# Sinkhorn attention and a residual MLP on one core: q of two batches turned by DMA transposes, v and k mixing moved to other slots, and the last output tile split by columns

## The chip, the core and the metric

The kernel runs on one core of one Trainium2 chip. A core has TensorE (PE, the matmuls; PEld is its weight load), VectorE (DVE), ScalarE (ACT), GpSimd (POOL) and SyncE (SP), which here only issues DMAs. Each works through its own instructions in order and waits on semaphores for the others. The DMAs that SyncE, ScalarE and GpSimd issue are carried out by the core's 16 DMA engines. The metric is the time of one execution on the device in microseconds. Eight runs of the kernel before have a median of 276.93 us (276.42 to 279.34).

## What is computed

Four batches of 768 positions go through an attention with 8 heads of 64, whose blocks of keys and values are first mixed by an 8x8 matrix per head (five Sinkhorn rounds of a softmax over rows and columns), and then through a token mixing layer and a channel MLP, both with residuals:

```python
    P = sort_net
    for _ in range(5):
        P = np.exp(P - np.max(P, axis=-1, keepdims=True))
        P = P / (np.sum(P, axis=-1, keepdims=True) + 1e-09)
        P = P / (np.sum(P, axis=-2, keepdims=True) + 1e-09)
    k_sorted = np.einsum('bhij,bhjcd->bhicd', P, k_b)      # 8 blocks of 96 positions
    v_sorted = np.einsum('bhij,bhjcd->bhicd', P, v_b)
    # within each block i of 96 queries, keys and values:
    attn = softmax(scale * q_b @ k_sorted^T)
    x = attn @ v_sorted                                    # (4, 768, 512) over all heads
    a1 = alpha1 * x + beta1
    u = x + lam * einsum('ts,bsd->btd', w_tok, a1)         # token layer
    a2 = alpha2 * u + beta2
    out = u + lam * (np.maximum(a2 @ w_ch1, 0.0) @ w_ch2)  # channel layer, 512 -> 2048 -> 512
```

(The first lines are put together from the reference's steps; the arithmetic is the reference's.) Inputs and output are float32. The kernel works in 16-bit formats with float32 sums.

## The kernel before

**The order is written out by hand.** Every engine object is wrapped so that its instructions keep the order in which the program issues them (class `Engine`, L55 to L71); SyncE's DMAs alone are issued without the wrapper. The backbone is the loop at L859: for each batch b and each half hf of its 768 positions there is an *h phase* and then a *c phase*. I write h(b,hf) and c(b,hf). An h phase has 16 units (`h_unit`, L692): four matmuls give a 128x384 tile of the hidden layer, and ACT applies Relu and writes it to `hTa` or `hTb`. A c phase has three output tiles kk of 128 positions, each in four quarters of four matmuls (`ch_unit`, L695); after the last quarter DVE multiplies by `lamB`, GpSimd (for the last half of batch 3, DVE) adds `u`, and SyncE writes the tile to `out` in two DMAs, of 96 and of 32 rows. The tile goes through `ost`, which has two buffers, shared over the whole kernel.

**All other work hangs on this backbone.** `put(b, hf, kind, n, ...)` (L791) notes a piece of work for after unit n of a phase (n runs to 15 in an h phase and to 11 in a c phase), and `run` issues it there, in the order in which it was noted. While batch p = b-1 passes through the channel layer, batch b's attention and token layer are made:

- `load_kv(b)` and `load_q(b)` on GpSimd's queue: four DMAs of v and k (6 KB pieces into `raw`, two buffers) and six of q (`qn`, one buffer), all with a change of type.
- `mix_matrix(b)`: one small matmul (`repv_ps`) and six DVE operations give the mixing matrices.
- `mix_v(b, n)`, three times: two matmuls each into `mix_ps`, and a copy of 128x1024 into `mixed`. `bounce_v(b)` writes `mixed` to DRAM in two DMAs, and `back_v(b)` reads it back into `Vs` with positions on partitions, in pieces of 128 bytes.
- `mix_k(b, n)`, three times: eight matmuls into `kmix_ps`, and four casts into `kT`, on ACT or DVE.
- `q_turn_late(b, g)`, four times: six PE transposes of `qn` into `qt_ps` and a copy into `qT`.
- `score(b, g, hf)`, eight times: eight matmuls into `sc_ps`, and an exp on ACT into `et`. `pv(b, g, hf)`, eight times: eight matmuls into `x_ps`, a reciprocal and a multiplication on DVE into `x`; the first affine step of the token layer (`a1 = alpha1*x + beta1`, two DVE operations) is kept back in the list `late` and issued by `flush`.
- `tails(b)`: six small DVE copies that move the last quarter of the positions onto partitions 96 to 127. `moe_tok(b, kt)`, six times: six matmuls and three elementwise operations (`toktmp`, `u16`, and `u` in float32 on GpSimd). `moe_cross(b, hf)`: three DMA transposes of `u16` into `uT` on SyncE's queue. `moe_affine(b, hf)`: four DVE operations that give `a2T`, what the next h phase multiplies.

PSUM is held by two pools: `psA` (two buffers of two banks: scores, pv, mixing of v and k, `repv_ps`) and `psB` (four buffers of one bank: h, ch, tok and qt tiles). A tile takes the buffer that was freed first in program order, so a matmul can wait for the last reader of an earlier tile of any kind in that pool.

In the kernel before, batch b's v is mixed in h(b-1,0), k is mixed and q turned in c(b-1,0), the scores of batches 2 and 3 run from quarter 8 of c(b-1,0) into h(b-1,1), one to three pieces at a slot, and the first three token tiles stand together in c(b-1,1).

Of the kernel before, what the change touches and what calls it, by code (L numbers as in the profile page):

```python
# [7 lines left out]
FT = mybir.dt.float32  # L8
F16 = mybir.dt.float16
# [7 lines left out]
def kernel(  # L17
# [56 lines left out]
    dve = Engine(nc.vector)  # L74
    act = Engine(nc.scalar)
    pool = Engine(nc.gpsimd)

    dram = ctx.enter_context(tc.tile_pool(name="dram", bufs=1, space=bass.MemoryType.DRAM))
    wts = ctx.enter_context(tc.tile_pool(name="wts", bufs=1))
# [9 lines left out]
    def psb(shape, dtype, name):  # L89
        return pools["psB"].tile(shape, dtype, name=name, tag="psB")  # L90
# [263 lines left out]
    def mix_matrix(b):  # L354
        mix_values(b, psa)
        big = att.tile([128, 2, H * NB], F16, name="bigM", tag="bigM", bufs=3)
        dve.tensor_tensor(
            big[:], bigV[b][:].rearrange("p h i -> p (h i)").unsqueeze(1).to_broadcast([128, 2, H * NB]),
            mth[:].unsqueeze(2).to_broadcast([128, 2, H * NB]), ALU.mult,
        )  # L360
        bigM[b] = big
        bgp = att.tile([128, 2, 2, H4, NB], F16, name="bigP", tag="bigP", bufs=3)
        for th in range(2):
            dve.tensor_tensor(
                bgp[:, :, th, :, :], bigV[b][:].rearrange("p (g a) i -> p a g i", a=2),
                mth[:, th:th + 1].unsqueeze(2).unsqueeze(3).to_broadcast([128, 2, H4, NB]), ALU.mult,
            )
        bigP[b] = bgp
# [91 lines left out]
    def pv(b, g, hf):  # L460
        if g == 0 and hf == 0:
            x_of[b] = moep.tile([128, 8, C], F16, name="x128", tag="x128", bufs=2)
            a1_of[b] = moep.tile([128, 8, C], F16, name="a1", tag="a1", bufs=1)
        ps = psa([128, 2, 512], FT, "x_ps")[:].rearrange("p a (k d) -> p a k d", d=128)
        et = ets[(b, g, hf)][:].rearrange("p a i t -> p (a i t)")
        for ii in range(4):
            for h2 in range(2):
                lo = (4 * h2 + ii) * BLK
                w = min(128, 8 * BLK - lo)
                pe.matmul(  # L470
                    ps[0:w, h2, ii, 0:D + 1], et[0:BLK, lo:lo + w],
                    Vs[b % 2][0:BLK, (2 * g + h2) * NB + 4 * hf + ii, 0:D + 1], start=True, stop=True,
                )
        rc = att.tile([128, 2, 4], FT, name="rcb", tag="rc", bufs=3)
        dve.reciprocal(rc[0:BLK], ps[0:BLK, :, :, D])
        dve.tensor_tensor(
            x_of[b][0:BLK, 4 * hf:4 * hf + 4, g * 128:(g + 1) * 128].rearrange("p k (a d) -> p k a d", a=2),
            ps[0:BLK, :, :, 0:D].rearrange("p a k d -> p k a d"),
            rc[0:BLK].rearrange("p a k -> p k a").unsqueeze(3).to_broadcast([BLK, 4, 2, D]), ALU.mult,
        )  # L480
        flush()
        late.append(lambda: first_affine(b, slice(0, BLK), slice(4 * hf, 4 * hf + 4), slice(g * 128, (g + 1) * 128)))

    late = []

    def flush():
        while late:
            late.pop()()

    def tails(x, lo, hi, eng):  # L490
        flush()
        for a in range(3):
            eng(x[96:128, a:a + 4:3, lo:hi], x[32 * a:32 * a + 32, 6:8, lo:hi])

    def q_turn_late(b, g, eng):
        if g == 0:
# [45 lines left out]

    def bounce_v(b):
        for th in range(2):
            nc.sync.dma_start(
                vscr[b, :, th * HB:(th + 1) * HB, :], mixed[b][th * 64:(th + 1) * 64, :, :],
            )

    def back_v(b):
        nc.sync.dma_start(Vs[b % 2][0:BLK, :, 0:D], vscr[b].rearrange("x t d -> t x d"))  # L550

    w_tokT = const([128, NT, S], F16, "w_tokT")
    wp_of = {}
# [106 lines left out]
    def moe_cross(b, hf):  # L660
        uT = uT_of[(b, hf)] = att.tile([128, CT, 384], F16, name="uT", tag="uT", bufs=2)
        for m in range(3):
            nc.sync.dma_start_transpose(
                uT[:, :, m * 128:(m + 1) * 128], u16_of[b][:, 3 * hf + m, :],
            )

    def moe_affine(b, hf):
        for ci in range(CT):
            affine(b, hf, ci, uT_of[(b, hf)][:, ci, :], dve)
# [22 lines left out]
    def h_unit(b, hf, m):  # L692
        h_part(b, hf, m, range(CT))

    def ch_unit(b, hf, kk, part=(0, HT)):  # L695
        hT = hT_of[(b, hf)]
        kt = 3 * hf + kk
        if part[0] == 0:
            ch_of[0] = psb([128, C], FT, "ch_ps")
        cps = ch_of[0]  # L700
        for m in range(*part):
            pe.matmul(
                cps[:], hT[m][:, kk * 128:(kk + 1) * 128], W2p[:, m, :],
                start=(m == 0), stop=(m == HT - 1),
            )
        if part[1] < HT:
            return
        ost = att.tile([128, C], FT, name="ost", tag="ost", bufs=2)
        dve.tensor_tensor(ost[:], cps[:], lamB[:], ALU.mult)
        (dve if b == B - 1 and hf == 1 else pool).tensor_tensor(ost[:], ost[:], u_of[b][kt], ALU.add)  # L710
        act_out(out[b, kt * 96:(kt + 1) * 96, :], ost[0:96, :])
        act_out(out[b, TAIL + kt * 32:TAIL + (kt + 1) * 32, :], ost[96:128, :])

    ch_of = {}
    act_out = nc.sync.dma_start

    copy = dve.tensor_copy

# [72 lines left out]
    def put(b, hf, kind, n, *todo):  # L791
        at.setdefault((b, hf, kind, n), []).extend(todo)
# [6 lines left out]
        put(0, 0, "h", 4 + kt, lambda kt=kt: moe_tok(0, kt, psb))  # L799
    for ks in range(NT):  # L800
        put(0, 0, "h", ks, lambda ks=ks: prep_wtok(ks, 1, psb, (dve.tensor_copy, act.copy)[ks % 2]))
    for n in range(1, B):
        put(max(n - 2, 0), n > 1, *(("h", 10), ("c", 5))[n > 1], lambda n=n: mix_matrix(n))
    put(0, 0, "h", 9, lambda: moe_cross(0, 1))
    for g in range(CT):
        put(0, 0, "h", g, lambda g=g: first_affine(0, slice(0, 128), slice(0, NT), slice(g * 128, (g + 1) * 128)))
    for m in range(3):
        put(0, 0, "h", 10 + m, lambda m=m: first_back(m, psb))
    put(0, 0, "c", 3, lambda: moe_affine(0, 1))
    for b in range(1, B):  # L810
        p = b - 1
        off = 3 if b == 1 else 0
        for n in range(3):
            put(p, 0, "h", (13 if b == 1 else 10) + n, lambda b=b, n=n: mix_v(b, n, dve.tensor_copy))
        put(p, 0, "h", 15 if b == 1 else 12, lambda b=b: bounce_v(b))
        put(p, 0, "c", 4 if b == 1 else 0, lambda b=b: back_v(b))
        for n in range(3):
            put(p, 0, "c", off + 3 * n, lambda b=b, n=n: mix_k(b, n, ((act.copy, dve.tensor_copy)[n % 2],) * 4))
        for g in range(H4):
            put(p, 0, "c", off + (1, 4, 7, 7)[g], lambda b=b, g=g: q_turn_late(b, g, (dve.tensor_copy, act.copy, dve.tensor_copy, act.copy)[g]))  # L820
        if b + 1 < B:
            put(p, 0, "c", 11, lambda b=b: load_kv(b + 1), lambda b=b: load_q(b + 1))
        seq = [("s", 0), ("s", 1), ("s", 2), ("p", 0), ("s", 3), ("p", 1), ("p", 2), ("s", 4), ("p", 3), ("s", 5),
               ("p", 4), ("s", 6), ("p", 5), ("s", 7), ("p", 6), ("p", 7)]
        if b == 1:
            when = [("h", 0), ("h", 1), ("h", 2), ("h", 3), ("h", 4), ("h", 5), ("h", 6), ("h", 7), ("h", 8), ("h", 9),
                    ("h", 10), ("h", 11), ("h", 12), ("h", 13), ("h", 14), ("h", 15)]
        else:
            when = [("c", 8), ("c", 9), ("c", 10), ("c", 10), ("c", 11), ("c", 11), ("h", 0), ("h", 1), ("h", 2), ("h", 3),
                    ("h", 4), ("h", 5), ("h", 6), ("h", 8), ("h", 9), ("h", 11)]  # L830
        for (kind, n), (ph, at_) in zip(seq, when):
            f = (lambda b=b, n=n: score(b, n // 2, n % 2, psa)) if kind == "s" else (lambda b=b, n=n: pv(b, n // 2, n % 2))
            put(p, 1 if ph == "h" else 0, ph, at_, f)
        last = [("h", 12), ("h", 15)][b == 1]
        put(
            p, 1, *last, lambda b=b: tails(a1_of[b], 0, C, dve.tensor_copy),
            lambda b=b: tails(x_of[b], 0, C, dve.tensor_copy),
        )
        put(p, 1, "h", 4, lambda b=b: moe_start(b))
        for kt in range(3):  # L840
            put(p, 1, "c", 5 if b == 1 else 3, lambda b=b, kt=kt: moe_tok(b, kt, psb))
        put(p, 1, "c", 5 if b == 1 else 3, lambda b=b: moe_cross(b, 0))
        put(p, 1, "c", 8 if b == 1 else 7, lambda b=b: moe_affine(b, 0))
        for kt in range(3):
            put(b, 0, "h", 2 * kt, lambda b=b, kt=kt: moe_tok(b, 3 + kt, psb))
        put(b, 0, "h", 4, lambda b=b: moe_cross(b, 1))
        put(b, 0, "h", 13, lambda b=b: moe_affine(b, 1))

# [50 lines left out]
```

## Time and profile before

The profiled execution took 276.94 us, of which the span from the first to the last instruction is 275.1 us.

| engine | busy us | share of the span |
|---|---|---|
| PE, matmul | 260.7 | 95% |
| PE, weight load | 141.3 | 51% |
| DVE | 167.0 | 61% |
| ACT | 126.0 | 46% |
| POOL | 97.2 | 35% |

The granted TensorE clock is 0.998 of full speed over the span. A line of a group or of the timeline gives start, length, engine, the line of the recording helper (L65 for all wrapped engines), operation and tiles; in brackets stands the idle time of the engine before it and what ended it. Matmuls are pipelined, so their listed lengths overlap. SPq is SyncE's queue of DMA issues. In a row of windows the range in microseconds is followed by its length, then for each engine its busy time and number of instructions, then the granted clock, the share of the DMA engines (over 1 where packets overlap) and the bandwidth.

The phases around the change begin at: c(0,0) 59.7, h(0,1) 72.5, c(0,1) 88.4, h(1,0) 104.4, c(1,0) 120.4, h(1,1) 136.2, c(1,1) 150.4, h(2,0) 165.0, h(3,0) 224.8, the last c phase 260.1. The last matmul ends at 270.2.

### The profile page before, as it was taken

The numbers are of one execution on the slowest core, as the hardware profiler recorded it, in microseconds if no ns is written. First come the engines' busy times: TensorE is split into PE (matmuls) and PEld (weight loads), VectorE is DVE, ScalarE is ACT, GpSimd is POOL, SyncE is SP. The second block draws the span as 40 slices with busy tenths as digits, with TensorE's granted clock in tenths as the row PEclk, the third lists the DMA queues.
The fourth block names the chain that finished last, engine by engine and source line by source line (L and its number), as shares of the span: only waits on it lengthen the run. The fifth ranks groups of instructions, "written<-read, shape, count | busy, mean of one in ns | idle before, by whom it ended". The sixth has DMA issues, their size and how long they took to land.

```text
span 275.1 us, 5402 instructions
## 1 busy us (share of the span) xinstructions
PE 260.7 (95%) x2189; PEld 141.3 (51%) x2205; DVE 167.0 (61%) x345; ACT 126.0 (46%) x231; POOL 97.2 (35%) x104
## 2 busy tenths in 40 slices
PE   7998999999999998999999999999999999999992
PEld 2466555545556444556456445555465445545540
DVE  5788517987468985466398794555689755121042
ACT  2588557225787002565767003566774004605600
POOL 8637203601562185402282456203100746022000
PEclk9999999999999999999999999999999999999999
DMA  6999999999999333349479932159300223012012
GB/s 104 213 204 169 207 207 213 183 121 190 123 184 170 26 94 94 45 95 120 93 145 182 97 78 76 38 118 132 93 7 2 76 57 79 19 38 79 0 38 76
DMA packets 60684, 29.46 MB, mean 107 GB/s; under 512 B 50082, under 2 KB 56242, under 8 KB 60660
## 3 DMA queue, kind: packets, MB, share of 16 engines
q0 software_dynamic: 26352, 15.34, 39.9%
q1 hardware_dynamic: 34308, 13.79, 26.6%
q8 instruction: 17, 0.28, 0.4%
q14 instruction: 7, 0.06, 0.1%
HBM read 32.79 MB, written 8.65 MB: 151 GB/s over the span
## 4 chain that ended last, share of the span: by engine, by line
PE 78%; DVE 8%; DMA 5%; ACT 3%; issue 3%; POOL 1%; DVEq 0%; ACTq 0%; POOLq 0%
PE h_ps L65 29%; PE ch_ps L65 25%; PE tok_ps L65 10%; DMA v<-in_v_dram 4%; PE x_ps L65 3%; PE sc_ps L65 3%; DVE x L65 2%; ACT kT L65 2%; DVE a L65 2%; PE kmix_ps L65 1%; PE mix_ps L65 1%; PE v_ps L65 1%; DVE ost L65 1%; PE qt_ps L65 1%; PE turn_ps L65 1%
## 5 line engine op out<-in xcount | busy, mean ns | idle before, releaser
L65 PE MATMUL h_ps<-a2T,W1p 128*128 128x384 bf16 x512 | 96.0, 326 | 1.9 <-DVE a2T L65 1.5
L65 ACT ACTIVATE hTa<-h_ps 128x384 bf16<-128x384 f32 x96 | 47.0, 493 | 90.6 <-PE h_ps L65 90.4
L65 PE MATMUL ch_ps<-W2p,hTa 128*128 128x512 bf16 x274 | 67.2, 379 | 1.0 <-issue 0.3
L65 POOL TENSOR_TENSOR ost<-ost,u 128x512 f32<-128x512 f32 x21 | 26.6, 1267 | 114.6 <-DVE ost L65 109.5
L65 PEld LDWEIGHTS <-W1p 128*128 128x128 bf16 x512 | 47.3, 98 | 33.5 <-issue 2.5
L65 PEld LDWEIGHTS <-hTa 128*128 128x128 bf16 x288 | 27.1, 98 | 29.0
L65 DVE TENSOR_TENSOR ost<-ch_ps,lamB 128x512 f32<-128x512 f32 x24 | 16.6, 691 | 39.7 <-PE ch_ps L65 36.8
L65 POOL TENSOR_TENSOR u<-toktmp,x 128x512 f32<-128x512 f32 x18 | 29.3, 1641 | 8.9 <-DVE toktmp L65 8.9
L65 PE MATMUL tok_ps<-a,w_tokT 128*128 128x512 f16 x126 | 29.7, 379 | 0.0
L65 ACT ACTIVATE et<-sc_ps 96x768 f16<-96x768 f32 (+1 forms) x32 | 25.6, 810 | 2.6 <-PE sc_ps L65 2.6
L65 PE MATMUL ch_ps<-W2p,hTb 128*128 128x512 bf16 x94 | 24.4, 379 | 0.1
L65 DVE TENSOR_TENSOR toktmp<-tok_ps,lamB 128x512 f32<-128x512 f32 x21 | 14.4, 687 | 13.3 <-PE tok_ps L65 12.0
L65 ACT CAST kT<-kmix_ps 64x512 f16<-64x512 f32 x24 | 17.1, 713 | 10.0 <-PE kmix_ps L65 9.7
L65 ACT ACTIVATE hTb<-h_ps 128x384 bf16<-128x384 f32 x32 | 15.7, 491 | 9.7 <-PE h_ps L65 9.5
L65 PEld LDWEIGHTS <-w_tokT 128*128 128x128 f16 x126 | 12.2, 98 | 13.8 <-DVE a L65 0.4
L65 DVE TENSOR_TENSOR u<-toktmp,x 128x512 f16<-128x512 f32 (+1 forms) x24 | 17.8, 750 | 0.7
L65 POOL DMA_DIRECT2D qn<-in_q_dram x18 | 16.0, 924 | 5.0 <-DMA raw<-in_v_dram 5.0
L65 DVE TENSOR_TENSOR x<-x_ps,rcb 96x512 f16<-96x512 f32 x24 | 16.5, 687 | 0.8
L65 PE MATMUL x_ps<-Vs,et 96*128 96x65 f16 (+4 forms) x288 | 14.4, 195 | 2.0 <-DVE x L65 1.0
L65 PEld LDWEIGHTS <-et 96*128 96x128 f16 (+4 forms) x288 | 12.5, 100 | 6.8 <-DVE x L65 2.4
L65 DVE TENSOR_SCALAR a2T<-uT,ab2col 128x384 bf16<-128x384 f16 x28 | 11.7, 478 | 4.5 <-DMA uT<-u 4.4
L65 DVE RECIPROCAL rcb<-x_ps 96x8 f32<-96x8 f32 x24 | 4.8, 200 | 15.6 <-PE x_ps L65 15.4
(113 smaller groups left out, 255.3 us busy)
## 6 DMA issues: line engine op xcount, KB each, us to landing
out_dram<-ost SPq DMA_DIRECT2D x24, 192.0 KB, 2.3
raw<-in_v_dram POOLq DMA_DIRECT2D x6, 384.0 KB, 8.2
raw<-in_k_dram POOLq DMA_DIRECT2D x6, 384.0 KB, 9.5
qn<-in_q_dram POOLq DMA_DIRECT2D x18, 128.0 KB, 9.4
vscr<-mixed SPq DMA_DIRECT2D x6, 384.0 KB, 4.0
Vs<-vscr SPq DMA_DIRECT2D x3, 768.0 KB
W1p<-in_moe_w_ch_dram POOLq DMA_DIRECT2D x4, 512.0 KB, 13.5
W2p<-in_moe_w_ch_dram POOLq DMA_DIRECT2D x4, 512.0 KB, 17.4
```

Of the source, the lines that this page charges most:

```text
L65: ins = getattr(self.eng, name)(*args, **kwargs)
```

## The change

- q of batches 2 and 3 is turned by six DMA transposes each on SyncE's queue (`q_cross`), at quarters 6 to 11 of c(b-2,1), in place of 24 PE transposes and four copies each. Batch 1 keeps `q_turn_late`.
- For batches 2 and 3, `mix_v` (copies now on ACT), `bounce_v` and `mix_k` (all casts now on ACT) move to c(b-2,1), quarters 4 to 11; `back_v` goes to unit 6 of h(b-1,0), and so do `load_kv(b+1)` and `load_q(b+1)`, where there is a next batch. For batch 2's own load nothing changes.
- `mix_matrix(2)` moves from quarter 5 of c(0,1) to quarter 6 of c(0,0), `mix_matrix(3)` from quarter 5 of c(1,1) to unit 12 of h(1,0).
- Scores and pv of batches 2 and 3 go in pairs to fixed slots from unit 15 of h(b-1,0) to unit 4 of h(b-1,1), and `flush` runs one slot after each pair of pv.
- The first three token tiles of batch 1 stand at quarter 4 of c(0,1) (before: 5), those of batches 2 and 3 one each at quarters 0, 1 and 2 (before: all at 3), each with its transposes after the third.
- The last output tile is made in two halves of 256 columns with a PSUM tile each (`last_out`); ScalarE issues the DMAs of its 32 rows.
- SyncE is wrapped as the other engines are, so that its DMAs keep the program's order.

```diff
+    sp = Engine(nc.sync)
...
-        flush()
+        if b == 1:
+            flush()
...
-            late.pop()()
+            late.pop(0)()
...
+    def q_cross(b, kt):
+        if kt == 0:
+            qT_of[b] = att.tile([128, H4, S], F16, name="qT", tag="qT", bufs=1)
+        sp.dma_start_transpose(
+            qT_of[b][:, :, kt * 128:(kt + 1) * 128], qn_of[b][:, kt, :, :].rearrange("p h d -> p (h d)"),
+        )
...
+    def last_out(hT, cps, kk, kt):
+        for n in range(2):
+            c = slice(n * C // 2, (n + 1) * C // 2)
+            if n:
+                cps = psb([128, C // 2], FT, "ch_ps")
+                for m in range(HT):
+                    pe.matmul(
+                        cps[:], hT[m][:, kk * 128:(kk + 1) * 128], W2p[:, m, c],
+                        start=(m == 0), stop=(m == HT - 1),
+                    )
+            ost = att.tile([128, C // 2], FT, name="ost", tag="ost", bufs=2)
+            dve.tensor_tensor(ost[:], cps[:, 0:C // 2], lamB[:, c], ALU.mult)
+            dve.tensor_tensor(ost[:], ost[:], u_of[B - 1][kt][:, c], ALU.add)
+            sp.dma_start(out[B - 1, kt * 96:(kt + 1) * 96, c], ost[0:96, :])
+            nc.scalar.dma_start(out[B - 1, TAIL + kt * 32:TAIL + (kt + 1) * 32, c], ost[96:128, :])
...
-    for n in range(1, B):
-        put(max(n - 2, 0), n > 1, *(("h", 10), ("c", 5))[n > 1], lambda n=n: mix_matrix(n))
+    put(0, 0, "h", 10, lambda: mix_matrix(1))
+    put(0, 0, "c", 6, lambda: mix_matrix(2))
+    put(1, 0, "h", 12, lambda: mix_matrix(3))
...
+    pairs = [("s", 0), ("s", 2), ("p", 0), ("s", 4), ("p", 2), ("s", 6), ("p", 4), ("p", 6)]
...
+            for n in range(3):
+                put(p - 1, 1, "c", 4 + n, lambda b=b, n=n: mix_v(b, n, act.copy))
+                put(p - 1, 1, "c", 7 + 2 * n, lambda b=b, n=n: mix_k(b, n, (act.copy,) * 4))
+            put(p - 1, 1, "c", 7, lambda b=b: bounce_v(b))
+            put(p, 0, "h", 6, lambda b=b: back_v(b))
+            for kt in range(NT):
+                put(p - 1, 1, "c", 6 + kt, lambda b=b, kt=kt: q_cross(b, kt))
+            if b + 1 < B:
+                put(p, 0, "h", 6, lambda b=b: load_kv(b + 1), lambda b=b: load_q(b + 1))
+            for (kind, n), at_ in zip(
+                pairs, ((0, "h", 15), (0, "c", 1), (0, "c", 3), (0, "c", 6), (0, "c", 8), (0, "c", 11), (1, "h", 1), (1, "h", 4)),
+            ):
+                if kind == "p":
+                    put(p, at_[0], at_[1], at_[2] + 1, flush)
+                for i in range(2):
+                    f = (lambda b=b, n=n + i: score(b, n // 2, n % 2, psa)) if kind == "s" else (lambda b=b, n=n + i: pv(b, n // 2, n % 2))
+                    put(p, *at_, f)
...
-            put(p, 1, "c", 5 if b == 1 else 3, lambda b=b, kt=kt: moe_tok(b, kt, psb))
-        put(p, 1, "c", 5 if b == 1 else 3, lambda b=b: moe_cross(b, 0))
-        put(p, 1, "c", 8 if b == 1 else 7, lambda b=b: moe_affine(b, 0))
+            put(p, 1, "c", 4 if b == 1 else kt, lambda b=b, kt=kt: moe_tok(b, kt, psb))
+        put(p, 1, "c", 4 if b == 1 else 2, lambda b=b: moe_cross(b, 0))
+        put(p, 1, "c", 8 if b == 1 else 6, lambda b=b: moe_affine(b, 0))
```

More of the change, by code (lines that the diff above doesn't have):

```diff
@@ L544, in bounce_v @@
         for th in range(2):
-            nc.sync.dma_start(
+            sp.dma_start(
                 vscr[b, :, th * HB:(th + 1) * HB, :], mixed[b][th * 64:(th + 1) * 64, :, :],
@@ L549, in back_v @@
     def back_v(b):
-        nc.sync.dma_start(Vs[b % 2][0:BLK, :, 0:D], vscr[b].rearrange("x t d -> t x d"))
+        sp.dma_start(Vs[b % 2][0:BLK, :, 0:D], vscr[b].rearrange("x t d -> t x d"))
     w_tokT = const([128, NT, S], F16, "w_tokT")
@@ L662, in moe_cross @@
         for m in range(3):
-            nc.sync.dma_start_transpose(
+            sp.dma_start_transpose(
                 uT[:, :, m * 128:(m + 1) * 128], u16_of[b][:, 3 * hf + m, :],
@@ L700, in ch_unit @@
         cps = ch_of[0]
+        w = C // 2 if b == B - 1 and kt == NT - 1 else C
         for m in range(*part):
             pe.matmul(
-                cps[:], hT[m][:, kk * 128:(kk + 1) * 128], W2p[:, m, :],
+                cps[:, 0:w], hT[m][:, kk * 128:(kk + 1) * 128], W2p[:, m, 0:w],
                 start=(m == 0), stop=(m == HT - 1),
@@ L707, in ch_unit @@
             return
+        if b == B - 1 and kt == NT - 1:
+            return last_out(hT, cps, kk, kt)
         ost = att.tile([128, C], FT, name="ost", tag="ost", bufs=2)
@@ L714 @@
     ch_of = {}
-    act_out = nc.sync.dma_start
+    act_out = sp.dma_start
     copy = dve.tensor_copy
@@ L809 @@
     put(0, 0, "c", 3, lambda: moe_affine(0, 1))
+    pairs = [("s", 0), ("s", 2), ("p", 0), ("s", 4), ("p", 2), ("s", 6), ("p", 4), ("p", 6)]
     for b in range(1, B):
         p = b - 1
[L812 to L824, printed above, removed]
-        if b == 1:
-            when = [("h", 0), ("h", 1), ("h", 2), ("h", 3), ("h", 4), ("h", 5), ("h", 6), ("h", 7), ("h", 8), ("h", 9),
-                    ("h", 10), ("h", 11), ("h", 12), ("h", 13), ("h", 14), ("h", 15)]
-        else:
-            when = [("c", 8), ("c", 9), ("c", 10), ("c", 10), ("c", 11), ("c", 11), ("h", 0), ("h", 1), ("h", 2), ("h", 3),
-                    ("h", 4), ("h", 5), ("h", 6), ("h", 8), ("h", 9), ("h", 11)]
@@ L831 @@
[L831 to L834, printed above, removed]
+        if b == 1:
+            for n in range(3):
+                put(0, 0, "h", 13 + n, lambda n=n: mix_v(1, n, dve.tensor_copy))
+                put(0, 0, "c", 3 + 3 * n, lambda n=n: mix_k(1, n, ((act.copy, dve.tensor_copy)[n % 2],) * 4))
+            put(0, 0, "h", 15, lambda: bounce_v(1))
+            put(0, 0, "c", 4, lambda: back_v(1))
+            for g in range(H4):
+                put(0, 0, "c", (4, 7, 10, 10)[g], lambda g=g: q_turn_late(1, g, (dve.tensor_copy, act.copy)[g % 2]))
+            put(0, 0, "c", 11, lambda: load_kv(2), lambda: load_q(2))
+            seq = [("s", 0), ("s", 1), ("s", 2), ("p", 0), ("s", 3), ("p", 1), ("p", 2), ("s", 4), ("p", 3), ("s", 5),
+                   ("p", 4), ("s", 6), ("p", 5), ("s", 7), ("p", 6), ("p", 7)]
+            for at_, (kind, n) in enumerate(seq):
+                put(0, 1, "h", at_, (lambda n=n: score(1, n // 2, n % 2, psa)) if kind == "s" else (lambda n=n: pv(1, n // 2, n % 2)))
+        else:
+            for n in range(3):
+                put(p - 1, 1, "c", 4 + n, lambda b=b, n=n: mix_v(b, n, act.copy))
[14 more added lines that the diff above has]
+                    put(p, *at_, f)
@@ L835 @@
         put(
-            p, 1, *last, lambda b=b: tails(a1_of[b], 0, C, dve.tensor_copy),
+            p, 1, "h", 15 if b == 1 else 8, lambda b=b: tails(a1_of[b], 0, C, dve.tensor_copy),
             lambda b=b: tails(x_of[b], 0, C, dve.tensor_copy),
```

## The prediction, made before the changed kernel was run

> **What bounds it now.** I read the page's engine table first, then the windows by stage, then the chain of waits with the timeline around each wait on it, then the DMA windows of the two transfers that the change moves together.
>
> ```profile
> PE 260.7 (95%) x2189; PEld 141.3 (51%) x2205; DVE 167.0 (61%) x345; ACT 126.0 (46%) x231; POOL 97.2 (35%) x104
> ...
> PE 78%; DVE 8%; DMA 5%; ACT 3%; issue 3%; POOL 1%; DVEq 0%; ACTq 0%; POOLq 0%
> ```
> ```profile
> 88.39:104.35 15.96, 14.38 (x66) 6.36 (x66) 13.56 (x31) 0.22 (x1) 7.28 (x5) 1.00 0.49 62
> 104.35:120.42 16.07, 15.99 (x88) 8.60 (x88) 9.59 (x15) 7.32 (x15) 6.25 (x4) 1.00 0.30 59
> 120.42:136.17 15.75, 15.03 (x143) 8.44 (x144) 7.17 (x14) 10.31 (x16) 2.54 (x2) 1.00 0.87 134
> 136.17:150.37 14.20, 13.71 (x151) 8.20 (x147) 12.52 (x31) 10.31 (x20) 8.64 (x11) 1.00 0.94 148
> 150.37:165.01 14.64, 14.54 (x67) 6.55 (x68) 12.40 (x25) 0.53 (x2) 7.29 (x5) 1.00 0.79 91
> 165.01:224.78 59.77, 58.47 (x440) 31.70 (x443) 39.12 (x73) 28.46 (x50) 17.35 (x12) 1.00 0.35 67
> ```
> ```profile
> 104.35 0.73 PE L65 MATMUL h_ps<-a2T,W1p 128*128 128x384 bf16 x2 [1.53 <-DVE a2T L65]
> ...
> 131.63 0.34 PE L65 MATMUL sc_ps<-qT,kT 64*128 64x96 f16 x7 [0.46 <-ACT kT L65]
> ```
> TensorE carries the end; each window is one h or c phase (the sixth is batch 2's four), and its first number after the range is its length. Two of PE's own waits are worth a name: 1.53 us for a2T at 104.35, and 0.46 us for kT. The rest is what PE streams, so I price PE by distances between unit starts on the chain: an h unit 0.65 us, a quarter of a ch tile 0.864, a token tile 1.29, mix_v 0.43, mix_k 0.45, one q turn 0.335 (0.67 for two), a pv 0.26, a score 0.38 after other work and 0.28 after another score.
>
> The transfers (columns: length, clock, share of the DMA engines, GB/s):
> ```profile
> 124.93:126.00 1.07, 1.00 0.03 5
> 126.00:127.00 1.00, 1.00 1.14 180
> 127.00:128.00 1.00, 1.00 1.63 150
> ...
> 130.00:131.00 1.00, 1.00 1.68 138
> ```
> ```profile
> 80.00:82.00 2.00, 0.26 (x1) 1.00 1.00 203
> 82.00:84.00 2.00, 0.88 (x1) 1.00 1.02 206
> ...
> 86.00:88.00 2.00, 0.00 (x0) 1.00 2.36 154
> ```
> ```profile
> DMA to landing us min/median/max: 2.0/2.4/7.0
> ```
> The first is back_v(2), issued at 124.93 with the DMA engines to itself: full rate to about 131.6, so 6.7 us and some 7.0 to landing. The second is load_kv(2) and load_q(2), which fill the engines from about 76 to 91. The last line is the outputs': 2.4 us, but 7.0 where one was caught by such a load.
>
> **What the skill says.** "Trainium Kernel Development and Optimization", section Performance Expectations, calls matmul busy time a bad metric because matmuls are pipelined. The trace agrees: a 128x384 matmul is listed at 326 ns, yet four start within 0.65 us. "DMA: Bandwidth & Descriptors", section Issuing engines are not separate DMA queues: DMAs from SyncE and GpSimd share the same 16 engines. Its section Queues, rings and completion order: each engine takes turns between queues, a whole packet at a time. The 7.0 us above agrees with waiting behind packets of the other queue; how large a packet of back_v's 128-byte pieces is, no run here shows. "ScalarE: Activation LUTs", section Step-by-step: what each phase is for, gives one element per cycle and lane whatever the function. Here 128x384 takes 493 ns and 128x768 820, so 128x1024 is an estimated 1.04.
>
> **The change, part by part**, in the program's order with each wait traced to the instruction that ends it.
>
> c(0,0), 59.7 to 72.5. mix_matrix(2) comes in at quarter 6: one small matmul, and about 1.75 us of DVE (0.22+0.22+0.53+0.29+0.44) ahead of mix_k's casts. kmix now takes the buffer that ACT frees at 66.36, where PE came at 66.12. The later casts still end before h(0,1) needs them. Cost 0.25.
>
> c(0,1). Before: 12x0.864=10.37, tokens 3.88, wait 1.53, odds 0.2. After: tokens a quarter earlier, with the 2.1 us of mix_matrix gone from the DVE queue ahead of them. The third u16 is then ready at about 99.4 instead of 101.5, uT lands near 102, a2T ends near 103.5; PE arrives only at 105.5, since three mix_v (1.29) and three mix_k (1.35) for batch 2 now stand here. 10.37+3.88+1.29+1.35=16.89 against 15.96: +0.93. The six q transposes on the SP queue (1.19 us of issue each, median landing 2.3, as uT's) stand behind uT and before h(1,1)'s uT; they are not needed until scores at 121. Cost none, 0.5 if SP's backlog delayed the bounce, which has 15 us to spare.
>
> h(1,0). mix_v leaves; two scores (0.66) and a repv (0.15) come: 10.4+3.88+0.81=15.1. But all twelve kT casts now run on ACT (0.72 each, 8.64) in front of the first Relu. First kmix ends 4.36 us before h starts (two mix_k, four quarters), so ACT reaches that Relu 0.2+8.64-4.36=4.5 after h's start and ends it at 5.0. The second token tile needs that Relu's PSUM buffer, and PE is there after 0.65+1.29+0.65+0.65=3.24. A new wait of about 1.9; bounds 1.5 to 2.4, by how soon after its kmix ACT starts.
>
> c(1,0). No mix_k, no q turns; six scores in pairs (1.98), four pv (1.04): 13.4, against 15.75. Checked at each pair: exp (0.81 twice) and x (0.2+0.69 twice) end before the buffer's next use, two to three quarters on. h(1,1): 10.4+4x0.26=11.44 against 14.20. Moving flush a slot on leaves DVE some 2 us ahead of the tokens. c(1,1): 10.37+3.88+2.64=16.9 against 14.64. Batch 1's four phases: 15.1+1.9+13.4+11.4+16.9=58.7 against 60.66, so -1.9 to -2.0.
>
> Batch 2: no batch 4 to prepare, no repv. 14.95+1.9+13.4+11.44+14.25=55.9 against 59.77: -3.85. Of these -5.8 in all, 8x0.335=2.7 is q turns; the rest is gaps at scores and DVE waits of the old interleaving.
>
> The last tile. Two halves of 256 columns stream as long as one of 512. DVE falls from 0.69 to an estimated 0.42 per operation (687 ns at 512 columns, 957 at 768), and ACT issues one DMA. But ost has two buffers: the second half takes the one of the tile before, whose output, by the same 1.4 of DVE, issue and 2.4 of landing, arrives about 0.75 after the last matmul. So -0.2 of the 4.9 us tail; bounds +0.3 to -0.9. SP's order in the program is what it already was: nothing.
>
> Sum: 0.25+0.93-1.95-3.85-0.2=-4.8. Against the profiled run's own 276.94 us (span 275.1 and 1.84 around it; the median of 8 is 276.93) that is 272.1.
>
> **The term that is not in the trace.** back_v(2) and load_kv(3), load_q(3) now have the same slot, h(1,0) unit 6. Let T be the end of the last token tile. DVE needs 1.85 for u16; the third uT transpose 1.2; Vs is issued at T+3.1, packets from T+4.3, alone landed by T+10.1. GpSimd's u add ends at T+2.55; the v load issues then and its packets start near T+4. The first pv, c(1,0) quarter 3, needs Vs at T+12.0 (eleven h units 7.15, repv 0.1, four quarters 3.46, four scores 1.32). So there are 1.9 us of slack, and the load holds the engines for 15. Let S be the wait at that pv, with every engine queued behind PE. Bounds: S is not below 0, and at most about 12, if Vs moves only once the loads are nearly through. If a turn is a partition row (64 pieces, 0.92 us by Vs's rate) against one 6 KB load packet (0.47), six turns cost about 3.8 us more and S is near 1.9. Equal time gives about 4, turns of 16 pieces 7 to 10. I take 1.9. For batch 3 there is no load, and S is 0.
>
> **Rivals.** *No wait* (0.20): Vs starts at once and gets ahead; for it, the first load packets are slow to start; against it, the 7.0 us output. 272.1. *Forecast* (0.36): S of 0.8 to 3.4, 272.9 to 275.5. *The gain is given back* (0.17): equal shares, S of 3.4 to 6.2, 275.5 to 278.3. *Slower* (0.27): the load packets starve Vs. Place: the first pv of batch 2; price up to 12; it decides from S above 4.8+1.4=6.2; time 278.4 to 284, about 281. For it, Vs is 6144 small pieces and the v and k loads go first; against it, the loads' 6 KB packets are few (16 per engine). A fifth, that DMA crossbars cost PE something, I give nothing: uT's transposes beside loads landed at worst in 4.3.
>
> **Numbers.** The predicted time is 276.94-4.8+1.9=274.0. The range of 8 in 10 runs from 271 (no wait, a better tail) to 281 (S of 9); the likeliest case alone 272.9 to 275.5. Half a per cent, 1.4 us, is about what a measurement can tell from no change: faster (below 275.5) 0.56, same 0.17, slower (above 278.3) 0.27.
>
> **What would show it.** Right: no a2T wait at h(1,0); a wait of 1.5 to 2.4 for a Relu before the second token tile of h(1,0) and of h(2,0); c(1,0) and h(1,1) near 13.4 (plus S) and 11.4; one wait of PE for the Vs DMA, about 2 us, in batch 2 only; batch 2's four phases near 56. Wrong: S above 6 turns the sign; no Relu wait would bring 3.8 more; a wait for qT would mean that the crossbars matter.

## The result, and the profile after

The changed kernel takes 287.85 us (median of 11 runs, 286.95 to 291.29) against 277.19 for the kernel before (32 runs): a ratio of 1.0377, 95% interval 1.0354 to 1.04. It is slower by some 10.5 us. The forecast was 274.0, in a range from 271 to 281. A few executions are slower than the rest of the same kernel; the medians count them, the ratios leave them out. The profiled execution took 288.4 us and has a span of 286.6, against 275.1.

Three parts of its page: the engine table, the chain that ended last by engine, and the DMA issue of Vs (count, size, median us from issue to landing).

```profile
PE 259.0 (90%) x2157; PEld 141.4 (49%) x2173; DVE 148.6 (52%) x329; ACT 134.5 (47%) x241; POOL 97.4 (34%) x104
...
PE 74%; DMA 11%; ACT 7%; DVE 3%; issue 2%; SPq 2%; DVEq 0%
...
Vs<-vscr SPq DMA_DIRECT2D x3, 768.0 KB, 20.7
```

TensorE's busy time hardly moved (260.7 before), but its share of the span fell from 95% to 90%. One transfer, which had no row of its own on the chain before, now takes a tenth of the span. The waits of TensorE (total, times, longest):

```profile
PE x_ps L65 <- DMA Vs<-vscr: 13.9, 2, 12.8
PE tok_ps L65 <- ACT hTa L65: 3.5, 2, 1.8
```

Stage by stage, the windows of TensorE after (first number after the range: length; then busy time of each engine, clock, DMA share, GB/s) are, in this order, h(1,0), c(1,0), h(1,1), c(1,1), and batch 2's four phases together:

```profile
105.42:122.43 17.01, 15.22 (x102) 8.29 (x99) 5.82 (x13) 12.05 (x23) 11.48 (x12) 1.00 0.72 145
122.43:151.46 29.03, 15.91 (x130) 7.54 (x130) 9.27 (x22) 4.63 (x8) 4.67 (x5) 0.76 1.00 112
151.46:162.80 11.34, 11.34 (x96) 7.23 (x97) 9.52 (x24) 8.50 (x17) 1.27 (x1) 1.00 0.09 25
162.80:179.71 16.91, 16.80 (x96) 8.39 (x96) 6.88 (x13) 7.67 (x11) 7.48 (x5) 1.00 0.36 70
179.71:236.58 56.87, 53.80 (x387) 28.64 (x390) 29.72 (x64) 25.66 (x47) 17.52 (x12) 1.00 0.41 75
```

Nearly all the loss is in the second row. c(1,0) was to take 13.4 us plus the wait; it took 29.03, of which TensorE was idle for 12.8, and its mean clock was 0.76. TensorE's timeline at that place (start, length; in brackets the idle time before and what ended it), and then the clock in short windows around it (clock, DMA share, GB/s are the last three columns):

```profile
139.40 1.09 PE L65 MATMUL x_ps<-Vs,et 96*128 96x65 f16 x16 [12.79 <-DMA Vs<-vscr]
140.31 1.47 PE L65 MATMUL ch_ps<-W2p,hTa 128*128 128x512 bf16 x3
142.00 3.62 PE L65 MATMUL ch_ps<-W2p,hTa 128*128 128x512 bf16 x8 [0.22 <-issue]
```
```profile
130.00:132.00 2.00, 0.00 (x0) 0.99 2.01 145
132.00:134.00 2.00, 0.00 (x0) 0.50 2.01 145
...
142.00:144.00 2.00, 2.00 (x5) 0.50 0.00 0
144.00:146.00 2.00, 2.00 (x20) 0.60 0.00 0
146.00:148.00 2.00, 2.00 (x21) 1.00 0.00 0
```

The wait is 12.79 us, and it does something more: by 132.0 the TensorE clock has halved, and it comes back at about 145.6 (in the row with 0.60, 1.6 of 2 us are at half speed). Eight ch matmuls, less than 1.8 us at the chain's 0.864 us for four, take 3.62. "TensorE: Matmul & The Clock Gate" in the Trainium skill, Part 1, says that an idle window of some 3.4 us halves the clock and a busy one of that length restores it. The trace agrees in kind; here the clock fell 5.3 us after the last matmul and came back 6.2 us after the next.

The cause stands in the DMA packets of three windows, from 118 to 124 us, from 124 to 128 and from 129 to 138. The first row of each is GpSimd's queue with the loads, the second SyncE's, with Vs from 124.3 on (packets, MB, share):

```profile
q0 software_dynamic: 142, 0.77, 80.8%
q1 hardware_dynamic: 545, 0.13, 11.5%
```
```profile
q0 software_dynamic: 162, 0.80, 96.5%
q1 hardware_dynamic: 162, 0.02, 5.9%
```
```profile
q0 software_dynamic: 5120, 0.65, 109.0%
q1 hardware_dynamic: 5120, 0.66, 91.7%
```

In the second and third window the two queues take turns one for one, packet against packet: 162 to 162, then 5120 to 5120. The turns are single pieces, not runs of them: in the half microsecond from 125.0 to 125.5, about as long as one 6 KB packet takes (0.47 us), each queue has 16 packets, as many as there are DMA engines. In the second window the load's packets are 6 KB (v and k) and Vs's are its 128-byte pieces, so Vs gets 0.02 MB in 4 us. In the third, q's own pieces are 128 bytes too, and each side gets half.

The first window holds no piece of Vs at all, though Vs was issued at 118.59. SyncE's 0.13 MB are the 512 pieces of 256 bytes of the third uT transpose, which stands ahead of Vs on the same queue and moves only between 121.3 and 122.8; 545 to 142 is not one for one, and what held that transpose back until 121.3 is not shown. The first piece of Vs moves 5.7 us after the issue; in the run below with the loads moved away, it is 1.2 us. So of the 12.7 us by which Vs lands later than in that run (20.7 against 8.0), about 4.5 go to waiting behind the transpose, 3.7 to the turns with the 6 KB packets, and the remaining 4.5 to the turns with q's pieces (an estimate from the times of the packets).

### The profile page after: what moved, and what is told of

The parts are those of the page before. It is cut to its first block, busy times and chain, and to the rows that moved or that the text cites. A ratio compares the mean times of both kernels' runs of the same rounds, so it can differ in the third digit from the quotient of the medians.

```text
span 286.6 us, 5358 instructions
## 1 busy us (share of the span) xinstructions
PE 259.0 (90%) x2157; PEld 141.4 (49%) x2173; DVE 148.6 (52%) x329; ACT 134.5 (47%) x241; POOL 97.4 (34%) x104
## 4 chain that ended last, share of the span: by engine, by line
PE 74%; DMA 11%; ACT 7%; DVE 3%; issue 2%; SPq 2%; DVEq 0%
PE ch_ps L65 24%; PE h_ps L65 23%; DMA Vs<-vscr 10%; PE tok_ps L65 10%; ACT kT L65 6%; PE x_ps L65 4%; PE warm_ps L65 4%; PE sc_ps L65 2%; SPq L65 2%; PE mix_ps L65 1%; PE v_ps L65 1%; DVE ost L65 1%; PE turn_ps L65 1%; PE wtok_ps L65 1%; DMA out_dram<-ost 1%
## 5 line engine op out<-in xcount | busy, mean ns | idle before, releaser
L65 PE MATMUL h_ps<-a2T,W1p 128*128 128x384 bf16 x512 | 92.0, 326 | 0.3 <-ACT a2T L65 0.3
L65 PE MATMUL ch_ps<-W2p,hTa 128*128 128x512 bf16 (+1 forms) x287 | 70.5, 380 | 0.9 <-issue 0.2
L65 PEld LDWEIGHTS <-W1p 128*128 128x128 bf16 x512 | 48.2, 98 | 31.8 <-issue 0.2
L65 PEld LDWEIGHTS <-hTa 128*128 128x128 bf16 x300 | 28.9, 100 | 30.6 <-issue 2.8
L65 DVE TENSOR_TENSOR ost<-ch_ps,lamB 128x512 f32<-128x512 f32 (+1 forms) x25 | 16.7, 668 | 48.2 <-PE ch_ps L65 46.7
L65 ACT ACTIVATE et<-sc_ps 96x768 f16<-96x768 f32 (+1 forms) x32 | 24.8, 811 | 34.2 <-PE sc_ps L65 34.2
L65 PE MATMUL x_ps<-Vs,et 96*128 96x65 f16 (+4 forms) x288 | 13.5, 198 | 15.1 <-DMA Vs<-vscr 13.9
L65 ACT CAST kT<-kmix_ps 64x512 f16<-64x512 f32 x32 | 22.9, 715 | 6.3 <-PE kmix_ps L65 5.6
L65 PE MATMUL ch_ps<-W2p,hTb 128*128 128x512 bf16 (+1 forms) x97 | 24.2, 370 | 0.2
L65 PEld LDWEIGHTS <-w_tokT 128*128 128x128 f16 x126 | 12.2, 98 | 17.8 <-issue 4.1
L65 DVE TENSOR_SCALAR a2T<-uT,ab2col 128x384 bf16<-128x384 f16 x28 | 10.0, 420 | 15.1 <-DMA uT<-u 15.1
## 6 DMA issues: line engine op xcount, KB each, us to landing
Vs<-vscr SPq DMA_DIRECT2D x3, 768.0 KB, 20.7
W1p<-in_moe_w_ch_dram POOLq DMA_DIRECT2D x4, 512.0 KB, 13.3
```

Source lines behind the costliest of these rows:

```text
L65: ins = getattr(self.eng, name)(*args, **kwargs)
```

## Experiments

Theory A: the loads for the next batch, in the same slot as Vs, hold Vs up by taking a turn for each of its small pieces (as first put, without the transpose ahead of it). Rival B: Vs is late by its slot and by what stands ahead of it on SyncE's queue, whatever the loads do. All ratios are to the kernel before on the same chip (two chips, on which it has medians of 276.9 and 277.2).

**The loads later, together and apart.** In the first run both loads move, in the second only q's, in the third only those of v and k.

```diff
-put(p, 0, "h", 6, lambda b=b: load_kv(b + 1), lambda b=b: load_q(b + 1))
+put(p, 0, "c", 11, lambda b=b: load_kv(b + 1), lambda b=b: load_q(b + 1))   # both
```

> Both loads of the next batch issue at the last quarter of c(1,0) instead of unit 6 of h(1,0); Vs keeps its slot. Theory A (packets of the loads hold up Vs's 128-byte pieces): Vs of batch 2 lands 8.8 us after its issue, as Vs of batch 3 did, so PE waits about 0.8 us at the first pv in place of 12.8, the TensorE clock does not fall, and the time is 273 us. Rival B (Vs is late by its slot and by what stands ahead of it on the SyncE queue, whatever the loads do): PE still waits 8 us or more, time above 283.

> Only the q load issues later (last quarter of c(1,0)); the v and k loads stay in Vs's slot. Theory A with turns of one packet each: Vs hardly moves beside the 6 KB packets of v and k, which end near 128.3 us, then runs alone for 6.7 us: it lands near 135.5, PE waits about 9, time 284. If the q load alone were the harm: wait 1, time 273. Rival B: no change, 287.9.

> Only the v and k loads issue later; the q load stays in Vs's slot. Theory A with turns of one packet each: q's 128-byte pieces and those of Vs alternate, so Vs takes some 10.5 us instead of 6.7: it lands near 131, PE waits about 4 to 4.5, the clock may or may not fall, time 276 to 278. If only the 6 KB packets were the harm: wait 1, time 273. Rival B: no change, 287.9.

Measured, in that order: 272.98 us (ratio 0.9833, 0.9787 to 0.988), 282.59 (1.0186, 1.0125 to 1.0248) and 279.93 (1.0094, 1.0065 to 1.0123). TensorE's wait for Vs in the three (total, times, longest):

```profile
PE x_ps L65 <- DMA Vs<-vscr: 1.5, 2, 1.1
```
```profile
PE x_ps L65 <- DMA Vs<-vscr: 9.0, 2, 8.4
```
```profile
PE x_ps L65 <- DMA Vs<-vscr: 5.8, 2, 4.9
```

Moving one line turns the whole result: 287.85 becomes 272.98, and the changed kernel is then faster than the one before. Rival B falls as an account of the loss. Of the 12.5 us by which the batch-2 wait shrinks (12.8 to 0.3), moving q's load alone takes 4.4 and moving those of v and k alone 7.9: nearly the sum, and the shares estimated above.

The run with only q's load moved came out near its expectation (a wait of 8.4 for about 9, 282.6 for 284), but not in the way that theory A had it. One line of its trace from VectorE's timeline, and one with the packets of SyncE's queue from 128 to 133 us:

```profile
128.69 1.25 DVE L65 TENSOR_SCALAR a2T<-uT,ab2col 128x384 bf16<-128x384 f16 x4 [7.86 <-DMA uT<-u]
```
```profile
q1 hardware_dynamic: 5300, 0.68, 167.3%
```

Here it is the third uT transpose that took turns with the 6 KB packets (between 121.0 and 126.5 us, 196 packets to the load's 219). Vs's first piece moved only at 126.9, from about 128 it had the DMA engines to itself, and it was through by 133.4. So what the v and k loads hold back is SyncE's queue in its order, and the delay of what stands ahead is handed on to Vs.

In the run with q still beside Vs the time came out above what was expected (279.9 for 276 to 278), since a wait of 4.9 us was followed by a halved clock there too: full speed returned at about 136.6, 4.8 us after the pv at 131.80, which costs half of that. With this, 273.0 + 4.6 + 2.4 = 280.0.

**Vs earlier, the loads left.**

```diff
-put(p, 0, "h", 6, lambda b=b: back_v(b))
+put(p, 0, "h", 0, lambda b=b: back_v(b))
```

> The loads keep their slot; Vs of batches 2 and 3 issues at unit 0 of h(b-1,0) instead of unit 6. Theory A: Vs lands before the loads begin, PE waits for it in neither batch, no fall of the clock: 287.9 - 12.8 - 1.1 - 2.9 for the slow stretch = 271 us. Rival B gives the same here; a third theory, that the loads slow the outputs and crossbars of this stage as much as Vs, would leave waits of several us for a2T or ost, time above 275.

Measured: 282.09 us (1.0158, 1.0098 to 1.0217), not 271. Vs landed in 8.4 us and nobody waited for it. One line each from the chain of waits, from VectorE's timeline and from TensorE's timeline of this run:

```profile
122.96 12.84 DMA uT<-u
```
```profile
135.93 1.25 DVE L65 TENSOR_SCALAR a2T<-uT,ab2col 128x384 bf16<-128x384 f16 x4 [13.99 <-DMA uT<-u]
```
```profile
138.66 0.50 PE L65 MATMUL sc_ps<-qT,kT 64*128 64x96 f16 x8 [8.37 <-DVE x L65]
```

The third uT transpose is now behind Vs and takes the place of Vs as the victim: it lands after 12.84 us. VectorE sits at a2T with x's normalization queued behind it, and TensorE's next scores wait for the PSUM buffer that x frees; the clock halved again, from 135.2 to 142.1. This was the third theory in the text above. So it is not Vs that is at fault but whatever SyncE has in flight when the loads begin. In the changed kernel, too, that transpose comes first: VectorE begins a2T there at 125.04, after waiting 3.67 us for uT, and in the run with the loads moved at 121.25, with no wait.

**Vs in long pieces.** Is it the size of the pieces, or SyncE's queue as such?

```diff
-        sp.dma_start(Vs[b % 2][0:BLK, :, 0:D], vscr[b].rearrange("x t d -> t x d"))
+        if b == 1:
+            sp.dma_start(Vs[1][0:BLK, :, 0:D], vscr[1].rearrange("x t d -> t x d"))
+        else:
+            sp.dma_start(
+                Vs[b % 2][0:BLK].rearrange("p x d -> p (x d)")[:, 0:H * NB * D],
+                vscr[b].rearrange("x t d -> (x t d)").rearrange("(p f) -> p f", p=BLK),
+            )
```

> The changed kernel, the loads in their slot, but Vs of batches 2 and 3 fetched as 96 rows of 8192 bytes in one run each instead of 64 pieces of 128 bytes: as many bytes, in the same slot (the values are put elsewhere in Vs, over the column of ones too, so attention of these batches is not the reference's). Theory A (turns by pieces, so the small piece loses): Vs gets about half of the bytes, some 8 us, lands by 128, PE waits at most 1.5 us, no fall of the clock, time 273 to 274. Rival D (SyncE's ring as such is served behind GpSimd's until the loads end, whatever its pieces): the wait stays above 8 us, time above 283.

Measured: 278.21 us (1.0021, 1.0 to 1.0042). Vs lands in 12.2 us in place of 20.7, and the wait is 4.33 instead of 12.79. In its window from 124 to 128 us, Vs's queue and that of the loads:

```profile
q1 hardware_dynamic: 65, 0.53, 57.7%
q0 software_dynamic: 64, 0.29, 35.9%
```

Turns are still one for one, 65 to 64, but now Vs's queue moves 0.53 MB in the time in which it moved 0.02. That is what theory A says. The time was 4 us above the expected 274. The third uT transpose, still in 256-byte pieces, went ahead on the same queue: VectorE began a2T at 124.62, after waiting for uT, and the first row of Vs moved only at 123.85, 5.6 us after its issue. And the clock, which was not to fall, was halved from 131.1 to 134.6, which costs half of that. Rival D (SyncE's queue as such comes last) falls.

**Is the halved clock TensorE's idleness?** Matmuls of zeros ahead of the first pv of batch 2, first 48, then 62.

```diff
+if (b, kind, n) == (2, "p", 0):
+    put(p, *at_, lambda: warm(48))
```

> The changed kernel with 48 matmuls of zeros (128x512, some 10.3 us of TensorE) ahead of the first pv of batch 2, in the middle of the wait for Vs. Theory C (the halved TensorE clock after the wait is TensorE's own idleness): the clock stays at 1.00, the remaining wait is about 2.5 us, the pv still starts near 139.4, c(1,0) is 2.5 to 2.9 us shorter, time 285. Rival (the clock falls for another reason, or the loss lies elsewhere): 287.9, with the clock at 0.50 again.

> As the run with 48 matmuls of zeros, but 62 of them (some 13.4 us), so that they cover the whole wait for Vs, or nearly. Theory C: no idleness over a microsecond, so the clock stays at 1.00 through c(1,0), and c(1,0) is 2.5 to 2.9 us shorter than in the changed kernel, unless Vs itself lands later; time 285 to 286. Rival (the clock falls whatever TensorE does, or the fills hold back Vs): a stretch at 0.50 again, or Vs more than 22 us from issue to landing, and no gain.

Measured: 289.49 us (1.0422, 1.0378 to 1.0466) and 287.68 (1.0322, 1.0266 to 1.0377). The totals show no gain that can be told from no change, where 285 and 285 to 286 were expected; in both profiled runs Vs took 21.5 us to land instead of 20.7, and the stages before it had ended later. The traces say more. With 48 (clock is the third column from the end):

```profile
136.00:138.00 2.00, 1.55 (x8) 0.49 (x5) 0.00 (x0) 0.00 (x0) 0.00 (x0) 1.00 2.01 144
138.00:140.00 2.00, 0.00 (x0) 0.00 (x0) 0.00 (x0) 0.00 (x0) 0.00 (x0) 1.00 1.81 220
140.00:142.00 2.00, 1.00 (x19) 0.79 (x20) 0.51 (x2) 0.00 (x0) 0.00 (x0) 1.00 0.10 21
142.00:144.00 2.00, 2.00 (x6) 0.66 (x5) 1.93 (x6) 0.00 (x0) 0.00 (x0) 0.50 0.00 0
```

and with 62, TensorE's timeline and the clock:

```profile
141.84 0.67 PE L65 MATMUL x_ps<-Vs,et 96*128 96x65 f16 x16 [0.69 <-DMA Vs<-vscr]
142.57 2.53 PE L65 MATMUL ch_ps<-W2p,hTa 128*128 128x512 bf16 x11
```
```profile
142.00:144.00 2.00, 1.94 (x23) 1.13 (x21) 1.64 (x5) 0.00 (x0) 0.00 (x0) 1.00 0.00 0
```

With the whole wait filled the clock stays at 1.00, and eleven ch matmuls take 2.53 us, where eight took 3.62. From that pv to the end of the span are 144.5 us (286.3 - 141.84), against 147.2 in the changed kernel (286.6 - 139.40): 2.7 us less. That is the price of the halved clock here, and it is TensorE's idleness that brings it: filled, the wait leaves the clock alone. With 48, an idle gap of only 3.45 us brought the halving after work had resumed.

**What is left of the wait: SyncE's queue.** The next three runs start from the kernel with the loads later. One adds the early Vs, one gives the middle mix_k's casts back to VectorE, one issues q's crossbar transposes six quarters earlier.

```diff
+put(p, 0, "h", 0, lambda b=b: back_v(b))                                                   # Vs early
+put(p - 1, 1, "c", 7 + 2 * n, lambda b=b, n=n: mix_k(b, n, ((act.copy, dve.tensor_copy)[n % 2],) * 4))  # casts shared
+put(p - 1, 1, "c", kt, lambda b=b, kt=kt: q_cross(b, kt))                                   # crossbars early
```

> Loads later and Vs at unit 0 of h(b-1,0). If the last 0.3 and 1.1 us of waiting for Vs are only Vs's own length: they go, 271.5. Rival: with Vs ahead of it on the ring, the third uT transpose is late and x waits behind a2T on VectorE, 273 or more.

> Loads later, and the middle mix_k of batches 2 and 3 cast by VectorE, as in the kernel before. If ScalarE's twelve casts are what holds the first Relu (1.8 us of PE's wait in each of h(1,0) and h(2,0)): both waits go, 269.5. Rival: VectorE's four casts delay the third u16, and PE waits for a2T at the start of h(1,0) instead, 271.5 or more.

> Loads later, and the six crossbar transposes of q six quarters earlier (quarters 0 to 5 of c(b-2,1) instead of 6 to 11), nothing else. Theory E: SyncE comes to the third uT transpose when its u16 is ready, so Vs issues near 116.5 instead of 118.8, no wait for Vs is left: 271.6. Rival (Vs is held by the third u16, not by the queue): Vs at 118.8 as before, no change, 273.0.

Measured: 272.18 (0.9813, 0.976 to 0.9866), 274.11 (0.9849, 0.9789 to 0.991) and 271.28 (0.9769, 0.9735 to 0.9802). The early Vs took the waits for Vs off TensorE's list, but gained 0.8 us, not 1.5, and within the intervals that is no sure difference. The shared casts were a miss, and a useful one: by the ratio there is no difference from the run with the loads later alone, where 269.5 had been expected. TensorE's waits for a Relu did go (3.5 to 0.5 us), but the waits for Vs rose from 1.5 to

```profile
PE x_ps L65 <- DMA Vs<-vscr: 4.3, 2, 2.6
```

Neither theory had said this: PE came earlier and Vs did not. Over 100 to 130 us the chain of waits of this run stands, by line, at

```profile
by line: SPq L65 45.3%; DMA Vs<-vscr 26.5%; PE ch_ps L65 10.8%; ACT kT L65 9.6%; issue 3.5%; PE x_ps L65 2.2%; DVE ost L65 1.7%; PE mix_ps L65 0.7%
```

and SyncE's own timeline in it (the first transposes of q, an output, q's last, uT's three, then Vs) runs almost without a gap:

```profile
105.59 7.02 SPq L65 DMA_TRANSPOSE qT<-qn  x4
112.70 1.00 SPq L65 DMA_DIRECT2D out_dram<-ost  x2
113.79 1.21 SPq L65 DMA_TRANSPOSE qT<-qn  x1
115.08 3.83 SPq L65 DMA_TRANSPOSE uT<-u  x3
118.97 0.57 SPq L65 DMA_DIRECT2D Vs<-vscr  x1
```

Vs leaves at 118.97 since SyncE is still issuing crossbar transposes. With these six quarters earlier, Vs left at 117.55 instead of 118.78, no wait for its DMA remained in TensorE's list, and the median is 1.7 us lower (the two intervals just overlap; the 1.5 us of waiting that went are seen in the traces). SyncE's queue it was, though Vs left a microsecond later than the expected 116.5: SyncE now pauses between its last three transposes (issued at 111.50, 113.66 and 116.25).

**q on TensorE again, loads later.**

```diff
-put(p - 1, 1, "c", 6 + kt, lambda b=b, kt=kt: q_cross(b, kt))
+put(p - 1, 1, "c", 8 + g, lambda b=b, g=g: q_turn_late(b, g, (dve.tensor_copy, act.copy)[g % 2]))
```

> Loads later, and q of batches 2 and 3 turned by TensorE again (four turns each, in c(b-2,1), casts by VectorE and ScalarE in turn) instead of by the crossbars. Theory E (the crossbars cost TensorE nothing, but 9 us of SyncE's queue ahead of Vs): eight turns of 0.335 us come back, 2.7, the waits for Vs go, -1.4: 274.3 against 273.0. Rival: the queue costs nothing, +2.7 or more with the casts, 275.7; or the crossbars cost more than they bring, 273 or less.

Measured: 274.51 us (0.9885, 0.985 to 0.9919), 1.5 above the run with the loads later alone. The waits for Vs went, as expected, but in h(1,0) and h(2,0) TensorE now waits, with h and token tiles, behind ScalarE's copies of q:

```profile
PE h_ps L65 <- ACT qT L65: 3.0, 2, 1.5
PE tok_ps L65 <- ACT qT L65: 0.8, 2, 0.4
```

These 3.8 us stand where the Relu waits of 3.5 stood, so the turns (+2.7) and the lost Vs waits (-1.5) remain: +1.5 with the 0.3. The intervals of the two runs overlap, so it is the traces that carry this sum.

**Together.** Loads at quarter 5 of c(1,0), crossbars and Vs early, casts shared, the second half of the last tile in a buffer of its own:

```diff
-ost = att.tile([128, C // 2], FT, name="ost", tag="ost", bufs=2)
+ost = att.tile([128, C // 2], FT, name="ost", tag=("ost", "toktmp")[n], bufs=2)
```

> Loads at quarter 5 of c(1,0), q's crossbars at quarters 0 to 5, Vs at unit 0 of h(b-1,0), the middle mix_k cast by VectorE, and the second half of the last tile in a buffer of its own. Theories A and E and the cost of ScalarE's casts together: 273.0 less 1.4 (Vs), 3.5 (Relu waits) and some 0.7 (last output): 267.5 to 268.5. Rival: VectorE, now with four casts in each of c(0,1) and c(1,1), is late for a2T or x, 270 or more.

Measured: 268.76 us (0.968, 0.9653 to 0.9707), a quarter of a microsecond above the expected range, 8.5 below the kernel before by its median and 19 below the changed one. TensorE's longest waits and the engine table:

```profile
PE warm_ps L65 <- DVE wz L65: 1.2, 1, 1.2
PE h_ps L65 <- DVE ost L65: 1.0, 1, 1.0
```
```profile
PE 256.4 (96%) x2157; PEld 140.8 (53%) x2173; DVE 155.8 (58%) x337; ACT 128.9 (48%) x233; POOL 96.6 (36%) x104
```

None of a microsecond or more is for a transfer or for a Relu any more. The tail from the last matmul to the end of the span is 4.2 us, against 4.6 in the changed kernel and 4.9 before. The parts were not tried one by one in this combination, and the slot of the loads is a new one, so what each is worth here is not shown.

## Why the prediction was wrong

Apart from the wait for Vs, the sum of the parts was right to within a microsecond. Term by term, as the prediction put them:

- c(0,0) and c(0,1): h(1,0) began at 105.42 instead of 104.35, +1.07 where +1.18 was forecast, with no wait for a2T.
- h(1,0): 17.01 where 15.1 + 1.9 was forecast; the Relu wait was 1.79, within 1.5 to 2.4.
- c(1,0) without its wait: 13.4 forecast. In the run with the loads later, where the wait is 0.3: 13.3.
- h(1,1) and c(1,1): 11.34 and 16.91 for 11.44 and 16.9.
- batch 2: 56.87 for 55.9, the excess being a wait of 1.1 for Vs.
- the last tile: 0.3 less, for 0.2. The second half did wait for an earlier output to land, 1.35 us, as was said.

The step that failed is "The term that is not in the trace", the size of S, the wait at the first pv of batch 2. It took "a partition row (64 pieces, 0.92 us by Vs's rate) against one 6 KB load packet" as the turn, and so S = 1.9. The turn is one piece against one packet, and S was 12.8, just past the upper bound of "about 12" that the same paragraph gave. The three sizes of turn that it listed (a row, 16 pieces, equal time) left out the simplest, one piece. "DMA: Bandwidth & Descriptors" in the Trainium skill, section Queues, rings and completion order, puts a typical packet at some 9 to 17 descriptors; here, measured, a turn was one piece of 128 bytes, and the measurement decides. But the size of the turn with the 6 KB packets is only some 3.7 us of the error. Further:

- Packets of Vs were put at T+4.3, some 1.2 us after the issue. They began 5.7 us after it, behind the third uT transpose, which the loads had held back: some 4.5 us. The fifth rival gave nothing for such a delay, since "uT's transposes beside loads landed at worst in 4.3"; with Vs ahead of it, one took 12.84.
- The turns were counted against the v and k packets alone. q's pieces, the same size as Vs's, follow them, and without them the wait is 4.4 us shorter.
- The 1.9 us of slack rested on a landing of 7.0 us. Without any load beside it Vs took 8.0, and TensorE came 8.0 after its issue (126.6 against 118.59): the slack was nil, which is also why batch 3, where S was to be 0, waited 1.1.
- What S was worth was put at S alone. The idle time also halved the clock: 2.7 us more.

In sum: 274.0 + 10.9 (S, 12.8 for 1.9) + 1.1 (batch 3) + 2.7 (clock) = 288.7, against 288.4 in the profiled run. The rival called "Slower" had the place and, but for the clock, the price (up to 284), and its mechanism, load packets that starve Vs, holds from 124.3 us on but leaves out the transpose; it was given 0.27. That DMA crossbars cost TensorE nothing does not hold for the third transpose of u, which is part of the wait. What q's transposes cost in the changed kernel cannot be told from its profile, where Vs comes twelve microseconds late. Once that wait is gone, SyncE's nine us of transposes of q are on the path, and some 1.5 us hang on their slot.

## What to carry to other kernels

Price a transfer in small pieces by its count of pieces, not by its bytes, where another queue is active: in these runs each piece waited for a whole packet of the other. Before a load and a transfer with a deadline are put in one slot, find out what else is in flight on the issuing queue (here a transpose ahead of Vs, whose delay Vs inherits) and give the load a slot after the deadline, even where its own result is wanted soon. A long wait on TensorE can cost more than itself: here the clock halved with every wait of 3.45 us or more, and with no wait for Vs of 2.6 or less.

## What the runs showed of the hardware

- Where the queues of GpSimd and SyncE both moved pieces, they alternated packet for packet in these windows: 162 to 162 (6 KB against 128 bytes), 5120 to 5120 (128 against 128), 64 to 65 (with 8 KB rows in place of Vs's pieces). One window stands apart, 142 to 545 from 118 to 124 us of the changed kernel, when the transpose passed the load.
- In the six runs in which TensorE sat idle for 3.45 to 12.8 us at batch 2's Vs or x, the clock halved 2.5 to 5.3 us after the last matmul, in two of them (gaps of 3.45 and 4.33 us) when work had already begun again. Full speed returned 3.4 to 6.2 us after work resumed. The length of one gap is not the whole rule: in the run with 62 matmuls of zeros the clock was also halved from 23.7 to 27.1 us, early in the kernel, where the longest single gap was 1.15 us. Why is not shown.
- A crossbar transpose of q or u holds SyncE for 1.2 us to issue, but the first one after the bounce of v held it for some 3 (3.1 with shared casts, at 105.59), and the first of u behind an early Vs for some 5.6, with or without the loads beside it. What they waited for there is not shown.
